# Two output stores cut into transfers of 112, 6, 6 and 4 rows

## The chip, the cores and the metric

The kernel runs on one core of one Trainium2 chip. The metric is the device time of one execution in microseconds. Before the change the median of three runs is 254.41 us (254.31 to 254.42). The profiled execution took 254.46 us; its span on the core, which all times in the trace count from, is 252.7 us, at a mean granted TensorE clock of 0.986 of full speed. Inputs and output lie in the chip's main memory; sixteen DMA engines carry data between it and the core's on-chip memory (128 partitions, one row each).

## The reference

Two stages are fused. The first is attention over channels: for each of four batches, q, k and v are 6400 x 256 in float32, and

```
qn = q / (norm over rows + 1e-6);  kn likewise
s  = kn^T @ qn / tau               # 256 x 256
a  = softmax(s)                    # along the last axis
x  = v @ a                         # 6400 x 256
```

The second is a mixture of eight low-rank adapters on the 25,600 rows of x: `logits = x @ w_gate`, the two largest of eight are chosen for each row and weighted with their softmax, and each chosen adapter e adds `w * ((x @ A[e]) @ B[e])`, of rank 16, to the row. The output is x plus these, 25,600 x 256 in float32, 26.2 MB.

## The kernel before, in words

A batch is called a quarter here. Its 6400 rows are spread over the 128 partitions, 50 consecutive rows to a partition (line 490: `out.rearrange("(b p c) d -> b p c d", b=B, p=P)`). So a column c of 0 to 49 is one chunk of 128 rows, and ten neighbouring columns of one partition are 10,240 consecutive bytes of the output.

**First pass of a quarter.** q and k come in three pieces of 17, 17 and 16 chunks, cast to bfloat16 by the loads themselves (`do_load`, L578, issued from GpSimd). `do_G` (L593, L597, L602) accumulates k^T q and, for part of the chunks, the squared norms in two accumulators on TensorE. For the other chunks ScalarE squares (`do_sq`, L615) and VectorE sums (L621). At the end of a quarter a short serial part makes the softmax: copies of the accumulator (L651), reciprocal root, scaling (L710), exponential on ScalarE (`do_exp`, L715), transposes (`do_aT_ps`, L729), and the products of the attention matrix with the gate and A (L742 to L757).

**Second pass of a quarter.** v comes in five pieces of ten chunks (0 to 4). For a piece, TensorE transposes v (L788), computes the gate and the adapters' first product (L812, or L826 and L879), VectorE makes the top-two weights, the weighted products are transposed (L902), and `do_Y` (L915, L920) accumulates `v @ a` and the adapters' second product for two chunks at a time. `do_Ye` copies each pair into a y tile of 128 x 10 x 256 floats (L769 on ScalarE, L771 on VectorE). There are seven y tiles, used in turn. When a piece is complete, `do_store` (L926) sends its y tile out from SyncE (L928). The last two pieces of the last quarter go in three stores each.

**Order.** A planner (`make_plan`, `Plan.run`) works through all steps with estimated durations and ranks, and writes down an order; the steps are then issued in that order, so each engine carries out its instructions in it and a step that waits holds up what stands behind it. Loads take buffers as they come free. Stores can be held back: `HOLD` (L409) names, for a quarter's piece, a load that must have landed first, and `do_hold` (L645) is a tiny transfer on SyncE that waits for that load. On SyncE the order at the first stores is: piece 2 of quarter 0 (not held), hold on k of quarter 1 piece 2, piece 1, piece 3, hold on k of quarter 3 piece 1, and then the others.

The planner sees a store as one step of fixed cost whatever transfers `do_store` makes of it.

Of the kernel before, what the change touches and what calls it, by code (L numbers as in the profile page):

```python
# [32 lines left out]
class Clock:  # L33


    WINDOW, FIRST, LOW, HIGH = 3.413, 0.31, 0.5, 0.8

# [3 lines left out]
    def at(self, t):  # L41
        w = max(0, int((t - self.FIRST) / self.WINDOW) + 1)
        while len(self.cold) <= w:
            share = self.busy[-1] / self.WINDOW
            self.cold.append(share < (self.HIGH if self.cold[-1] else self.LOW))
            self.busy.append(0.0)
        return w

    def took(self, t, us):

        end, w = t, self.at(t)
        while us > 1e-9:
            pace = 2.0 if self.cold[w] else 1.0
            step = min(us * pace, max(self.FIRST + w * self.WINDOW - end, 1e-6))
            self.busy[w] += step
# [5 lines left out]
    def idle(self, t):  # L61

        w = self.at(t)
        return t - self.FIRST - (w - 1) * self.WINDOW - self.busy[w] > self.SPARE

# [165 lines left out]
def make_plan(B, order, ahead):  # L231
# [150 lines left out]
    for b in range(B):  # L382
        for i in range(NP):
            x = pos["v", b, max(g for g, (i0, _) in enumerate(V) if i0 <= i)]
            parts = UNITS if b == B - 1 and i >= NP - FINE else ((0, PC),)
            for c, n in parts:
# [25 lines left out]

PARTS = {(0, 0): ((0, 2), (2, 15)), (0, 2): ((34, 8), (42, 8)), (3, 2): ((34, 8), (42, 8))}
FINE = 2
FIRST = 4
OFF = {(0, 0, 'k'), (0, 0, 'q'), (0, 1, 'q'), (0, 2, 'k'), (0, 2, 'q'), (0, 4, 'q'), (0, 5, 'q'),
        (0, 6, 'k'), (0, 6, 'q'), (0, 7, 'k'), (0, 8, 'q'), (1, 0, 'k'), (1, 0, 'q'), (1, 1, 'q'),
# [41 lines left out]
def kernel(  # L459
# [11 lines left out]
    nc = tc.nc  # L471

    B, N, C = q.shape
    P = 128
# [15 lines left out]
    out_v = out.rearrange("(b p c) d -> b p c d", b=B, p=P)  # L490
# [44 lines left out]
    held = {}  # L535
# [25 lines left out]
    def do_load(s, what, b, i, c, n):  # L561
        if what == "v":
            t, src, c0 = sb(s, "v", (b, i), [P, PC * max(n for _, n in V), C], BF16), v_v, c
        else:
            t = sb(s, "qk", (what, b, i), [P, max(n for _, n in QK), C], BF16)
            src, c0 = {"q": q_v, "k": k_v}[what], QK[i][0]
            if (b, c) == (0, 0):
                n = FIRST
                if "first" not in W:
# [6 lines left out]
        if (what, b, i) in (("q", 0, 0), ("k", 0, 0)):  # L576
            c, n = FIRST, c + n - FIRST
        nc.gpsimd.dma_start(t[:, c - c0:c - c0 + n, :], src[b, :, c:c + n, :])  # L578
# [346 lines left out]

    def do_store(s, b, i, c, n):  # L926
        lo = i * PC + c
        nc.sync.dma_start(out_v[b, :, lo:lo + n, :], held["y", (b, i), ""][:, c:c + n, :])  # L928


    do = dict(load=do_load, wts=do_wts, sq=do_sq, add=do_add, red=do_red, n2p=do_n2p, hold=do_hold, warm=do_warm, cast=do_cast, G=do_G, accs=do_accs, n2=do_n2, rsqrt=do_rsqrt, rq_ps=do_rq_ps, s=do_s,
              exp=do_exp, recip=do_recip, aT_ps=do_aT_ps, aT=do_aT, waA_ps=do_waA_ps, waA=do_waA,
              a=do_a, ZL=do_ZL, ZLe=do_ZLe, T=do_T, Te=do_Te, log=do_log, loge=do_loge, Z=do_Z, Ze=do_Ze, gzT=do_gzT,
              gzTe=do_gzTe, Y=do_Y, Ye=do_Ye, store=do_store)
    for name in ("m1", "eq1", "lm", "m2", "mask", "msum", "t", "th", "g2"):
        do[name] = gate_step(name)
# [50 lines left out]
```

## Time and profile before

| what | us |
|---|---|
| time, median of three | 254.41 |
| span of the profiled execution | 252.7 |
| TensorE busy | 217.8 (86%) |
| VectorE busy | 192.7 (76%) |
| ScalarE busy | 151.1 (60%) |
| packets of loads, as a share of sixteen DMA engines' span | 74.4% |
| packets of stores and other SyncE transfers, likewise | 26.1% |
| store of a whole piece (1280 KB), median from issue to landing | 16.7 |
| first store of quarter 0 (piece 2), issued | 76.65 |
| then piece 1, and piece 3, issued | 78.40, 89.74 |

How to read it. Busy times are totals over stages with different limits; a share of 86% does not say that the engine bounds every stage. PE is TensorE, DVE is VectorE, ACT is ScalarE, POOL is GpSimd, SP is SyncE. A line such as `ACT ssq L615 <- DMA qk<-in_q_dram: 3.8, 1, 3.8` says that ScalarE stood idle before instructions of line 615 until a DMA landed: 3.8 us in all, once, 3.8 at most. The chain lists start, duration and what ran or was waited for. A line of stretches gives, after the start and end, its length, the busy times of PE, of PE's weight loads, of DVE, ACT and POOL with counts, the granted clock, the mean busy share of the DMA engines and the GB/s they moved. Packets are what a DMA engine handles one after another; a landing is the mark that one DMA engine leaves when its part of a transfer has arrived.

### The profile page before, as it was taken

To read this page: it belongs to the slowest core of one execution; us is meant where nothing else is said; L and a number is where in the kernel's file an instruction comes from. 1 tells how busy PE (TensorE), PEld (TensorE's weight loads), DVE (VectorE), ACT (ScalarE), POOL (GpSimd) and SP (SyncE) were. 2 spreads that over 40 slices of the span, in tenths; PEclk is the share of its full clock that TensorE was granted. 3 is DMA by queue.
4 is the path that set the end of the run, shared out by engine and by line. 5 is a ranking of instruction groups with operands and counts; after the bars stand their busy time and mean duration, and the time that the engine had idled before them with its cause. 6 is when DMAs were issued, how large, how long until landed. Compare 5 with 4: busy or idle time off the path is not lost.

```text
span 252.7 us, 5852 instructions
## 1 busy us (share of the span) xinstructions
PE 217.8 (86%) x2357; PEld 193.0 (76%) x2357; DVE 192.7 (76%) x528; ACT 151.1 (60%) x269; POOL 27.1 (11%) x54
## 2 busy tenths in 40 slices
PE   0274995988999998689999999889999979999990
PEld 0162882876999996579899899779999769999980
DVE  0055589869899987588899899489898898889850
ACT  5454427546786543975667768362674846657671
POOL 7003010040002002000500100500000000000000
PEclk9998899999999999999999999999999999999997
DMA  8999999999999999999999999999999999999996
GB/s 251 217 217 209 211 223 208 217 218 215 215 217 241 303 305 298 224 213 221 210 215 220 215 217 217 211 212 313 317 251 353 322 341 317 337 392 415 404 408 249
DMA packets 11243, 66.70 MB, mean 264 GB/s; under 512 B 1360, under 2 KB 1744, under 8 KB 6608
## 3 DMA queue, kind: packets, MB, share of 16 engines
q0 software_dynamic: 6912, 38.80, 74.4%
q1 hardware_dynamic: 3968, 26.87, 26.1%
q10 hardware_dynamic: 336, 0.66, 0.8%
q8 instruction: 18, 0.29, 0.4%
q14 instruction: 9, 0.07, 0.1%
HBM read 78.91 MB, written 26.21 MB: 416 GB/s over the span
## 4 chain that ended last, share of the span: by engine, by line
PE 53%; DMA 32%; issue 5%; DVE 4%; ACT 2%; POOL 1%; POOLq 0%; DVEq 0%
DMA v<-in_v_dram 18%; PE Y_ps L915 13%; PE acc L593 10%; DMA qk<-in_q_dram 10%; PE Y_ps L920 6%; PE T_ps L788 5%; PE ZL_ps L812 5%; DMA qk<-in_k_dram 5%; PE gzT_ps L902 4%; PE acc L597 3%; PE acc L602 2%; PE Z_ps L879 1%; ACT a_exp L715 1%; DVE a_bf L763 1%; PE log_ps L826 1%
## 5 line engine op out<-in xcount | busy, mean ns | idle before, releaser
L593 PE MATMUL acc<-qk 128*128 128x256 bf16 x400 | 69.6, 282 | 17.0 <-DMA qk<-in_k_dram 9.4
L915 PE MATMUL Y_ps<-a_bf,vT 128*128 128x256 bf16 x400 | 60.0, 273 | 0.2 <-DVE acc_sb L710 0.2
L621 DVE TENSOR_TENSOR ssq<-ssq,sq 128x1280 f32<-128x1280 f32 (+1 forms) x27 | 43.4, 1606 | 19.6 <-ACT sq L615 19.6
L769 ACT COPY y<-Y_ps 128x512 f32<-128x512 f32 x79 | 46.2, 586 | 16.6 <-PE Y_ps L920 13.5
L593 PEld LDWEIGHTS <-qk 128*128 128x128 bf16 x400 | 34.2, 101 | 20.7 <-DMA qk<-in_k_dram 11.5
L615 ACT ACTIVATE sq<-qk 128x1280 f32<-128x1280 bf16 (+1 forms) x27 | 36.9, 1368 | 17.7 <-DVE ssq L621 16.6
L915 PEld LDWEIGHTS <-vT 128*128 128x128 bf16 x400 | 38.9, 98 | 4.7 <-issue 0.3
L920 PE MATMUL Y_ps<-ball,gzT 128*128 128x256 bf16 x200 | 38.2, 273 | 0.0
L597 PE MATMUL acc<-qk 128*128 128x128 bf16 x242 | 34.5, 224 | 0.0
L788 PE MATMUL T_ps<-ident,v 128*128 128x128 f32 x200 | 27.6, 274 | 0.6 <-DVE waA_sb L757 0.4
L769 ACT COPY vT<-T_ps 128x512 f32<-128x512 f32 (+1 forms) x44 | 21.2, 510 | 10.9 <-PE T_ps L788 10.5
L597 PEld LDWEIGHTS <-qk 128*128 128x128 bf16 x242 | 24.4, 101 | 3.5
L890 DVE TENSOR_TENSOR gz<-zl,gateg 128x256 bf16<-128x256 f32 x70 | 26.3, 445 | 0.3
L578 POOL DMA_DIRECT2D v<-in_v_dram x20 | 11.5, 576 | 133.7 <-PE T_ps L788 92.8
L788 PEld LDWEIGHTS T_ps<-ident,v 128*128 128x128 f32 x200 | 22.3, 141 | 1.6 <-DVE waA_sb L757 0.6
L602 PE MATMUL acc<-qk 128*128 128x128 bf16 x168 | 23.4, 222 | 0.0
L902 PE MATMUL gzT_ps<-ident,gz 128*128 128x128 f32 x100 | 20.9, 281 | 2.6 <-DVE gateg L868 1.4
L920 PEld LDWEIGHTS <-gzT 128*128 128x128 bf16 x200 | 19.6, 98 | 2.3
L812 PE MATMUL ZL_ps<-waA_sb,vT 128*128 128x136 bf16 x280 | 19.5, 223 | 1.7 <-DVE waA_sb L757 1.5
L771 DVE COPY gzT<-gzT_ps 128x256 f32<-128x256 f32 (+1 forms) x40 | 15.0, 380 | 7.1 <-PE gzT_ps L902 5.6
L812 PEld LDWEIGHTS <-vT 128*128 128x128 bf16 x280 | 17.7, 98 | 2.4 <-issue 2.1
L615 ACT ACTIVATE ssq<-qk 128x1536 f32<-128x1536 bf16 x8 | 11.9, 1489 | 11.4 <-DMA qk<-in_q_dram 7.4
(80 smaller groups left out, 271.3 us busy)
## 6 DMA issues: line engine op xcount, KB each, us to landing
out_dram<-y SPq DMA_DIRECT2D x18, 1280.0 KB, 16.7
v<-in_v_dram POOLq DMA_DIRECT2D x20, 640.0 KB, 20.5
qk<-in_q_dram POOLq DMA_DIRECT2D x7, 1088.0 KB, 23.7
qk<-in_k_dram POOLq DMA_DIRECT2D x7, 1088.0 KB, 28.4
qk<-in_q_dram POOLq DMA_DIRECT2D x4, 512.0 KB, 19.2
qk<-in_k_dram POOLq DMA_DIRECT2D x4, 512.0 KB, 22.5
qk<-in_q_dram POOLq DMA_DIRECT2D x2, 1024.0 KB, 19.4
qk<-in_k_dram POOLq DMA_DIRECT2D x2, 1024.0 KB, 23.8
```

The source lines that it names most:

```text
L593: nc.tensor.matmul(acc[ic][:, 0:256], kt[:, j, ic::CC], qt[:, j, :], start=c == 0, stop=False, skip_group_check=True)
L597: nc.tensor.matmul(acc[ic][:, 256:384], kt[:, j, ic::CC], kt[:, j, ic::CC], start=False, stop=False, skip_group_check=True)
L602: nc.tensor.matmul(acc[ic][:, 384:512], qt[:, j, ic * P:(ic + 1) * P], qt[:, j, ic * P:(ic + 1) * P], start=False, stop=c == NC - 1, skip_ ...
L615: nc.scalar.activation(out[:, 0:n, :], t[:, j:j + n, :], ACT.Square)
L621: nc.vector.tensor_tensor(out=t, in0=t, in1=held["sq", (w, b, g), ""][:, 0:n, :], op=OP.add)
L769: nc.scalar.copy(out, in_)
L788: nc.tensor.matmul(ps[:, j, :], vt[:, c + j, :].bitcast(FP32), W["ident32"], is_transpose=True, start=(j == 0), stop=(j == n - 1))
L812: nc.tensor.matmul(ps[:, j, :], vT_of(b, i, c + j)[:, :, ic], st[b]["waA"][:, ic, :], start=(j == 0 and ic == 0), stop=(j == n - 1 and ic ...
L890: nc.vector.tensor_tensor(out=pairs[:, h].rearrange("p c (e r) -> p c e r", e=E), in0=z[:, 2 * h:2 * h + 2, :].rearrange("p c (e r) -> p c ...
L902: nc.tensor.matmul(ps[:, j, :], pairs[:, j * P:(j + 1) * P], W["ident32"], is_transpose=True, start=(j == 0), stop=(j == n // 2 - 1))
L915: nc.tensor.matmul(ps[:, j, :], vT_of(b, i, c + j)[:, :, ic], st[b]["a"][:, ic, :], start=(j == 0 and ic == 0), stop=False, skip_group_che ...
L920: nc.tensor.matmul(ps[:, j, :], pair[:, :, j], W["B"], start=False, stop=(j == 1), skip_group_check=True)
```

## The change

Two stores of quarter 0, those of pieces 2 and 3, are each issued as four transfers: partitions 0 to 111, 112 to 117, 118 to 123 and 124 to 127. All other stores stay one transfer of 128 partitions. The same bytes go to the same places. The purpose is to alter how the rows of these two stores are shared out among the sixteen DMA engines.

```diff
 FINE = 2
+SPLIT, SHARES = {(0, 2), (0, 3)}, (112, 6, 6, 4)
 FIRST = 4
...
     def do_store(s, b, i, c, n):
         lo = i * PC + c
-        nc.sync.dma_start(out_v[b, :, lo:lo + n, :], held["y", (b, i), ""][:, c:c + n, :])
+        p = 0
+        for rows in SHARES if (b, i) in SPLIT else (P,):
+            nc.sync.dma_start(out_v[b, p:p + rows, lo:lo + n, :], held["y", (b, i), ""][p:p + rows, c:c + n, :])
+            p += rows
```

## The prediction

> **What bounds the kernel now.** First the page: the busy shares, the slices and the queues.
>
> ```profile
> PE 217.8 (86%) x2357; PEld 193.0 (76%) x2357; DVE 192.7 (76%) x528; ACT 151.1 (60%) x269; POOL 27.1 (11%) x54
> ...
> DMA  8999999999999999999999999999999999999996
> GB/s 251 217 217 209 211 223 208 217 218 215 215 217 241 303 305 298 224 213 221 210 215 220 215 217 217 211 212 313 317 251 353 322 341 317 337 392 415 404 408 249
> ...
> q0 software_dynamic: 6912, 38.80, 74.4%
> q1 hardware_dynamic: 3968, 26.87, 26.1%
> q8 instruction: 18, 0.29, 0.4%
> ```
>
> The DMA engines are busy in every slice from start to end; loads (q0) and stores (q1) add up to 100% of sixteen engines. TensorE follows at 86%. Slices 13 to 16 (76 to 101 us) stand out before 170 us with up to 305 GB/s: there the first three output pieces leave between loads. Second, the waits between 60 and 150 us, and the chain there:
>
> ```profile
> ACT ssq L615 <- DMA qk<-in_q_dram: 3.8, 1, 3.8
> ...
> PE aT_ps L729 <- ACT a_exp L715: 2.2, 1, 2.2
> ```
>
> ```profile
> 77.04 24.46 DMA qk<-in_q_dram
> 101.49 0.02 issue
> 101.52 1.48 ACT ssq L615
> 103.00 0.83 ACT a_exp L715 x2
> 103.83 0.05 issue
> 103.88 0.28 PE aT_ps L729 x2
> ```
>
> One load, q of quarter 2 piece 0, is issued at 77.04 and lands at 101.49. A squaring of ScalarE waits for it; the exponential of quarter 1 stands behind that squaring in the queue, and TensorE behind the exponential. It is the only DMA wait of over 0.7 us on a computing engine after 60 us. Third, the stretches at the end and the last pieces of the chain:
>
> ```profile
> 205.00:239.00 34.00, 32.55 (x396) 30.17 (x394) 29.77 (x99) 21.63 (x49) 1.03 (x2) 1.00 1.01 367
> 239.00:247.00 8.00, 7.77 (x71) 6.64 (x68) 4.20 (x13) 5.64 (x11) 0.00 (x0) 1.00 0.98 401
> ```
>
> ```profile
> 246.55 0.23 PE Y_ps L920 x2
> 246.78 0.02 issue
> 246.81 0.59 ACT y L769
> ```
>
> TensorE works to 246.78 and the DMA engines stay full (1.01, then 0.98): two limits run side by side. Which ends last is in the landing records: each transfer leaves sixteen, one for each DMA engine, without its number. The last store, issued at 247.42, lands first at 249.95 and last at 251.95. The first engines had nothing queued (2.53 us from issue); the latest had 2.00 us of older work before it. So **the end hangs on the latest DMA engine**, and TensorE has 2 us of room against it.
>
> Read through the run, these spreads show a steady skew. The v load issued at 53.27 lands over 79.13 to 81.20: twelve engines within 0.86 us, then 1.20, 1.26, 1.90 and 2.07. For q of quarter 2 the latest are 2.41, 3.10 and 3.28 after the first (98.22). For the large store issued at 233.23 the delays are 0, 0.26, 0.36, 0.45, 0.80, 1.10, then eight from 1.87 to 3.09, then 3.81 and 3.95. Six engines are early, two late. Lateness comes in jumps: the q8 packet at 30.37 (0.97 us) is followed by one engine of sixteen going from within 0.65 to 1.57.
>
> **What the skill says.** (1) "DMA: Bandwidth & Descriptors", "Why a DMA increments its semaphore by 16 and not by 1": a transfer uses k engines, the largest k up to 16 that divides its slowest dimension, on the SyncE path the lowest-numbered k. So 112 rows use all sixteen, seven rows each; 6 rows the engines 0 to 5; 4 rows 0 to 3. Every transfer before has sixteen landings; none shows a smaller k. (2) Same page, "Queues, rings and completion order": an engine alternates between the queues that hold work, packet by packet. The trace agrees: near 82 us packets of 5,120 bytes (v) and 10,240 bytes (store) take turns, 0.773 us a pair. (3) "Runtime: NRT & Kernel Launch", "Instruction fetch mechanics": instructions come by DMA in 16 KiB blocks; the trace has 18 packets of 16,384 bytes, 0.89 to 0.99 us each, the source of the jumps. (4) First page, "Latency and other measured facts": engines 7 and 15 are usually the slower ones. The trace has two latest engines, with no numbers to them.
>
> **The change part by part.** *Bytes:* none added. One row is one packet of 10,240 bytes; eight take 3.06 us (first landings at 232.63 and 235.69 of two stores), so 0.382 us each. Per split store, engines 0 to 3 get 7+1+1+1 = 10 rows instead of 8, engines 4 and 5 get 9, engines 6 to 15 get 7. For two stores: engines 0 to 3 **+4 rows, +1.53 us**; 4 and 5 +0.76; 6 to 15 **-2 rows, -0.76 us**.
>
> *Issues:* six more on SyncE at 0.33 to 0.58 us (the duration range of its store issues), about 2.2 us. Three delay the hold at 77.75 and the store at 78.40 by some 1.1 us; q1 still holds piece 2 until the landings at 86 to 88 us, so its rings stay fed. Three follow the store at 89.74; after them stands only the next hold, whose load lands at 166.87. Hidden both times. The new waits for a reused semaphore, by the order of instructions, are on transfers landed long before, or for the last small ones on piece 2 (87.7, wanted after 90). The compute copies that reuse a y buffer get four waits for one, on stores landed by about 106; those buffers are filled again only with later quarter 1 pieces. Zero. Six more completion writes of 0.02 us or less each: zero. The other engines keep their instruction order.
>
> *The load at 101.49:* stringing packets into sixteen rows (each starts where one ended), the two latest engines finish this load at 101.14 and 100.97, and at those same instants their last packet of quarter 0's stores. All 24 store packets lay ahead of it. With 22, the load ends 0.76 earlier there. The next engine lands at 100.63, store packets still waiting: alternation goes on, so rows more or fewer behind it do not move it. Landing 101.49 - 0.76 = 100.73, still later than 100.63. The squaring, exponential and TensorE move by the same 0.76: the 2.2 us wait shrinks. If the latest two are among engines 0 to 5, the load stays at 101.49, no worse.
>
> *Later loads:* k of quarter 2 piece 0 lands at 106.96 and is used by TensorE at 109.75; the v load landing at 110.0 is used at 113.06. On a loaded engine they come up to 1.53 later, inside 2.8 and 3.1 us. Beyond 110 us no computing engine waits over 0.7 us for a load.
>
> *The end:* between the last two large stores the latest landings lie 3.04 us apart (242.68, 245.72), the price of eight rows: no pause on the latest engine, where the first ones lie 4.63 apart. So its end moves by what its work moves. If the two latest (3.95, 3.81) are in 6 to 15: 251.95 - 0.76 = 251.19. Engines 0 to 3, if they are the early ones (up to 0.45), rise to 1.98; 4 and 5 (1.10) to 1.86; the middle falls to 2.33; the latest is 3.19 and still sets the end. Both limits move by 0.76, and TensorE had 2 us of room anyway.
>
> The unknown price is which engines are late. Its bounds: all late ones relieved, -0.76; the latest loaded, +1.53. I take -0.76: the skill puts the slow engines at 7 and 15, both relieved; the same handful stays early from 125 us on (four or five within 0.47), so lateness is not passed round evenly.
>
> **Rivals.** *A middle engine takes over:* one of engines 0 to 3 is from the group at 2.26 to 2.6. It rises to 3.8 to 4.1 against the old 3.95: -0.15 to +0.2, time 254.3 to 254.6, no change. For it: eight of sixteen are in the middle. Against: lowest-numbered engines would have to be spread over the groups. *A late engine is loaded (slower):* middle at 3.09 gives 4.62, +0.67, 255.1; the latest at 3.95 gives 5.48, +1.53, 255.9. For it: no record names an engine; if lateness were strewn at random, four loaded engines would seldom all miss the late ten. Against: the early group persists. *Hidden anyway:* TensorE's chain gains nothing and its tail sets the end: 254.4. Against it: the 2.00 us of queue on the latest engine at the last store.
>
> **How the numbers follow.** Forecast, late engines relieved: 254.41 - 0.76 = 253.65, say 253.7, chance 0.58. No change (middle engine or hidden) 0.20, at 254.3 to 254.6. Slower 0.22, of which 0.13 near 255.1 and 0.09 near 255.9. Range: a little under the full gain, 253.4, for packets that run otherwise in small transfers, up to 255.1, which leaves out the worst. Faster by over 0.2% (0.51 us) is below 253.90: the forecast, 0.58; slower is above 254.92: 0.22.
>
> **What would show it.** Right: q of quarter 2 lands near 100.7, the ScalarE wait shrinks from 3.8 to about 3.0, the large store near 233 us has its latest landing some 3.2 us after the old first one, and the last store's spread is below 2.0. Wrong: that spread grows with a single group of four late engines; or the load stays at 101.5; or the 112-row transfer's packets take longer than 0.40 us; or the 6-row transfers land on sixteen engines.

## The result, and the profile after

After the change the kernel takes 255.49 us (median of four runs, 255.41 to 255.56) against 254.41 before (four runs, 254.31 to 254.47). The ratio is 1.0043, with a 95% interval of 1.0025 to 1.006: slower by about 1.1 us. The forecast was 253.7, and the range ended at 255.1.

First the page of the kernel after the change: busy shares, slices, queues.

```profile
PE 217.7 (86%) x2357; PEld 192.7 (76%) x2357; DVE 192.8 (76%) x528; ACT 151.3 (60%) x269; POOL 27.0 (11%) x54
...
DMA  8999999999999999999999999999999999999994
GB/s 253 212 217 211 214 222 210 215 218 213 217 215 255 300 299 284 234 219 217 210 215 221 216 214 218 211 212 317 313 260 356 342 324 319 335 403 425 399 408 173
...
q1 hardware_dynamic: 4000, 26.87, 26.0%
q8 instruction: 18, 0.29, 0.4%
q14 instruction: 9, 0.07, 0.1%
```

The engines' work and the stores' bytes are as before; q1 has 32 packets more, which carry no data to speak of. What differs stands in the last slice: a DMA share of 4 tenths and 173 GB/s, where it was 6 tenths and 249. The kernel ends with most DMA engines idle. The stretches after the last matmul show how many are left at work. Before the change (the columns are those of the earlier table of stretches; the last two are the DMA share and GB/s):

```profile
247.00:250.00 3.00, 0.00 (x0) 0.00 (x0) 0.00 (x0) 0.39 (x1) 0.00 (x0) 0.86 0.96 383
250.00:251.50 1.50, 0.00 (x0) 0.00 (x0) 0.00 (x0) 0.00 (x0) 0.00 (x0) 0.50 0.27 104
251.50:254.00 2.50, 0.00 (x0) 0.00 (x0) 0.00 (x0) 0.00 (x0) 0.00 (x0) 0.50 0.00 1
```

And after it, with the two stretches that were shown of before at the head:

```profile
205.00:239.00 34.00, 32.55 (x395) 30.16 (x393) 29.77 (x100) 21.52 (x48) 0.91 (x2) 1.00 1.01 366
239.00:247.00 8.00, 7.65 (x69) 6.54 (x66) 4.08 (x13) 5.75 (x11) 0.00 (x0) 1.00 0.98 405
...
247.00:250.00 3.00, 0.00 (x0) 0.00 (x0) 0.00 (x0) 0.27 (x1) 0.00 (x0) 1.00 0.94 374
250.00:251.50 1.50, 0.00 (x0) 0.00 (x0) 0.00 (x0) 0.00 (x0) 0.00 (x0) 0.98 0.21 83
251.50:254.00 2.50, 0.00 (x0) 0.00 (x0) 0.00 (x0) 0.00 (x0) 0.00 (x0) 0.50 0.03 10
```

Until 247 us next to nothing has changed in these sums. After 251.5 a share of 0.03 of sixteen engines over 2.5 us is 1.2 us of work: one engine, busy alone to the end. The sixteen landings of the last store (issued at 247.42 before, 247.29 after) say the same:

```
before: 249.95 249.96 249.96 249.97 249.97 250.10 250.32 250.40 250.67 250.74 251.02 251.02 251.10 251.15 251.75 251.95
after:  249.83 249.84 249.87 249.91 249.94 249.96 249.99 250.07 250.20 250.36 250.76 250.93 251.06 251.16 251.35 252.91
```

Fifteen engines are done by 251.35, which is 0.60 before the old end. One comes at 252.91, 0.96 after it. TensorE had nothing to do with it; its last matmuls end at 246.66, where they ended at 246.78:

```profile
246.43 0.23 PE Y_ps L921 x2
246.66 0.02 issue
246.68 0.59 ACT y L770
```

The other part of the forecast, the load of q of quarter 2, can be read in the waits of 60 to 150 us and the chain there:

```profile
ACT ssq L616 <- DMA qk<-in_q_dram: 2.9, 1, 2.9
PE aT_ps L730 <- ACT a_exp L716: 1.4, 1, 1.4
```

```profile
77.01 23.63 DMA qk<-in_q_dram
100.64 0.02 issue
100.67 1.48 ACT ssq L616
102.15 0.83 ACT a_exp L716 x2
102.98 0.05 issue
103.03 0.28 PE aT_ps L730 x2
```

It lands at 100.64 instead of 101.49, and TensorE goes on at 103.03 instead of 103.88, as forecast. But the 0.85 us does not last. Between 160 and 175 us ScalarE now waits 2.4 us for a later load of q (0.7 before), and the chain of 155 to 200 us hangs on a load of k, which lands at 183.80 (182.94 before):

```profile
ACT sq L616 <- DMA qk<-in_q_dram: 2.4, 1, 2.4
```

```profile
159.91 1.55 POOL qk L579 x3
161.46 22.34 DMA qk<-in_k_dram
183.85 0.39 PE acc L594 x2
```

So both gains that were forecast were there: the two latest engines became earlier, and the first load landed earlier. A third thing outweighed them: one engine that was not the latest became so, by a wide margin.

### The profile page after: what moved, and what is told of

It reads as the page before. It is cut to its first block, busy times and chain, and to the rows that moved or that the text cites. A ratio compares the mean times of both kernels' runs of the same rounds, so it can differ in the third digit from the quotient of the medians.

```text
span 253.7 us, 5862 instructions
## 1 busy us (share of the span) xinstructions
PE 217.7 (86%) x2357; PEld 192.7 (76%) x2357; DVE 192.8 (76%) x528; ACT 151.3 (60%) x269; POOL 27.0 (11%) x54
## 4 chain that ended last, share of the span: by engine, by line
PE 45%; DMA 40%; issue 6%; DVE 3%; ACT 2%; POOL 1%; POOLq 0%; DVEq 0%
DMA v<-in_v_dram 17%; DMA qk<-in_k_dram 14%; PE Y_ps L916 12%; DMA qk<-in_q_dram 9%; PE acc L594 7%; PE Y_ps L921 6%; PE T_ps L789 5%; PE ZL_ps L813 4%; PE gzT_ps L903 4%; PE acc L598 2%; PE acc L603 1%; PE Z_ps L880 1%; POOL qk L579 1%; ACT a_exp L716 1%; PE log_ps L827 1%
```

## The experiments

The ratios below are to runs of the kernel before that were taken beside each kernel (medians 254.34 to 254.40 us); landings are those of one profiled execution each.

The theory after the result: one of the engines 0 to 3, which carry four rows more, was already nearly the latest. Rivals: the three more transfers of each split store (issues, completion writes) cost time by themselves; or the load on any low-numbered engine costs it.

**Splitting without shifting, and even sharing.** Two kernels split the same stores so that each engine gets the eight rows per store that it had before.

```diff
-SPLIT, SHARES = {(0, 2), (0, 3)}, (112, 6, 6, 4)
+SPLIT, SHARES = {(0, 2), (0, 3)}, (112, 16)            # first kernel
+SPLIT, SHARES = {(0, 2), (0, 3)}, (32, 32, 32, 32)     # second kernel
```

> Both stores go as 112 + 16 rows: two transfers each on all sixteen DMA engines, 7 + 1 rows to an engine, so every engine carries what it carried before the change. Theory (the end is set by the work of the latest DMA engine; with the change that is one of the loaded engines 0 to 3): no change from before, 254.3 to 254.6, load of q of quarter 2 at 101.5, last landing at 252.0. Rival, more transfers and issues cost: a third of the six extra ones, +0.36, 254.8. Rival, rows of a 112-row transfer run slower than those of a 128-row one: the whole +1.08, 255.5.

> Both stores go as four transfers of 32 rows, each on all sixteen engines: as many issues and completions as the change or more, but 8 rows to every engine as before. Theory: no change from before, 254.3 to 254.6. Rival, issues and completions cost: +1.08, 255.5. Rival, 112-row transfers are slow: 254.4.

Measured: 254.74 us for 112 and 16 rows (ratio 1.0015, 1.0008 to 1.0021) and 254.46 us for four times 32 (1.0004, 0.9996 to 1.0012). Four transfers of equal shares cost nothing that can be measured, so it is not the number of transfers. The 0.3 us of 112 and 16 is above the theory's range and nearer to the rival's 254.8, while its last landing (251.82) is not later than before (251.95). That rest comes after the last landing; the ledger below finds it there. In the waits of the kernel with four times 32:

```profile
ACT ssq L616 <- DMA qk<-in_q_dram: 2.4, 1, 2.4
...
PE aT_ps L730 <- ACT a_exp L716: 0.9, 1, 0.9
```

Here the load of q of quarter 2 lands at 100.02, earlier still than after the change, and TensorE's last matmul ends at 245.86, 0.9 us before that of the kernel before. The time stays the same. TensorE's chain does not set the end, then; and the early landing of that load does not need the two missing rows, since no engine has fewer rows here.

**More or fewer rows on the low engines.**

```diff
-SPLIT, SHARES = {(0, 2), (0, 3)}, (112, 6, 6, 4)
+SPLIT, SHARES = {(0, 2), (0, 3)}, (112, 8, 8)          # engines 0 to 7: +2 rows in all
+SPLIT, SHARES = {(0, 2), (0, 3)}, (112, 4, 4, 4, 4)    # engines 0 to 3: +6 rows in all
```

> Both stores as 112 + 8 + 8 rows: engines 0 to 7 get 9 rows a store (+0.76 us over two), engines 8 to 15 get 7 (-0.76). Theory: the loaded engine that set the end with +1.53 (last landing 252.9) now carries 0.76 less, so its last landing is 252.1 and the time 254.5 to 254.7, if none of the late engines is number 6 or 7; if one is, its 251.95 becomes 252.7 and the time 255.2, and the load of q of quarter 2 may stay at 101.5. Rival, issues cost: four of six extra, 255.1. Rival, slow 112-row transfers: 255.5.

> Both stores as 112 + 4 + 4 + 4 + 4 rows: engines 0 to 3 get 11 rows a store (+2.29 us over two), engines 4 to 15 get 7 (-0.76). Theory: the engine that sets the end with the change gets 0.76 more, last landing 253.7, time 256.2 to 256.4; the load of q of quarter 2 lands at 100.6 as with the change, so TensorE's part at 104 us is early although the end is later. Rival, issues cost: eight extra against six, 255.8. Rival, the end follows the computing chain: no later than with the change.

Measured: 254.62 us (1.0012, 1.0004 to 1.002) and 256.21 us (1.0076, 1.0062 to 1.0089). The end of the second, in its stretches:

```profile
250.00:251.50 1.50, 0.00 (x0) 0.00 (x0) 0.00 (x0) 0.00 (x0) 0.00 (x0) 0.79 0.26 102
251.50:254.00 2.50, 0.00 (x0) 0.00 (x0) 0.00 (x0) 0.00 (x0) 0.00 (x0) 0.50 0.05 20
```

0.05 of sixteen engines over 2.5 us is 2.0 us, again about one engine alone; the last two landings are 252.23 and 253.52, and the other fourteen are in by 251.15. From four rows more on engine 3 (the change, 252.91) to six (253.52) the last landing moves by 0.61 us, 0.3 us a row where a packet's price is 0.382.

**Each store alone.**

```diff
-SPLIT, SHARES = {(0, 2), (0, 3)}, (112, 6, 6, 4)
+SPLIT, SHARES = {(0, 2)}, (112, 6, 6, 4)    # first kernel
+SPLIT, SHARES = {(0, 3)}, (112, 6, 6, 4)    # second kernel
```

> Only piece 2 of quarter 0 goes as 112 + 6 + 6 + 4 rows. Theory (work of the latest engine): the engine that sets the end with the change carries +0.76 instead of +1.53, last landing 252.0 to 252.2, time 254.5 to 254.7: most of the loss is gone, not half of it, since the unloaded late engines end at 251.6 to 252.0 anyway. Rival (each split store costs by itself): half of the loss, 254.95.

> Only piece 3 of quarter 0 goes as 112 + 6 + 6 + 4 rows. Theory: as with piece 2 alone, 254.5 to 254.7. Rival (each split store costs by itself, and the one that runs beside more loads costs more): about 254.95, and different from piece 2 alone.

Measured: 254.81 us (1.0019, 1.0012 to 1.0026) and 254.76 us (1.0016, 1.001 to 1.0023). Both lie just above the theory's range and below the rival's 254.95. The two differ by less than their intervals, so which store is split does not matter. Their loss of 0.35 to 0.40 us is mostly not that of the rows: 112 and 16, which moves no row, loses 0.33 as well, and all three lose 0.31 to 0.37 us after the last landing (the ledger below). So two rows more cost little (last landings 252.22 and 251.70, against 251.95) and four rows 0.96 us: the loaded engine had some room. An estimate of it from the landings is 1.53 - 0.96 = 0.57 us for four rows, and 2.29 - 1.57 = 0.72 us for six.

**Which engine is which.** A kernel gives nearly every engine another number of rows. Each packet of an engine starts where its last one ended, so the packets of the trace can be strung into sixteen rows, and the counts of output packets then give each string its engine. The numbers rest on the rule that the prediction takes from the Trainium skill in its first point, that a transfer of fewer engines takes the lowest-numbered ones; were it another order, the names would change and not the argument.

```diff
-SPLIT, SHARES = {(0, 2), (0, 3)}, (112, 6, 6, 4)
+SPLIT = {(0, 2): (96, 11, 6, 5, 4, 3, 2, 1), (0, 1): (64, 15, 14, 13, 12, 10), (0, 3): (96, 9, 8, 8, 7)}
...
-        for rows in SHARES if (b, i) in SPLIT else (P,):
+        for rows in SPLIT.get((b, i), (P,)):
```

> Three stores of quarter 0 (pieces 2, 1 and 3) are cut so that no two DMA engines get the same rows: 96+11+6+5+4+3+2+1, 64+15+14+13+12+10 and 96+9+8+8+7. A transfer of k rows below 16 uses engines 0 to k-1, so the rows that an engine carries tell its number in the trace. Not meant to be fast: engine 0 gets 8 rows more than before (+3.06 us), engine 15 eight fewer. Theory: the 8,192-byte instruction packets go to engines among 0 to 3 and the 16,384-byte ones to eight engines of which at most one is among 0 to 5; time 255.5 to 257. Rival (lateness is passed round all engines): instruction packets on every engine.

Measured: 256.12 us in one run. The instruction packets, strung up to 165 us, lie so:

```
16,384 bytes (q8): 30.1 engine 13, 48.7 engine 14, 61.4 engine 5, 76.1 engine 6, 85.4 engine 9, 96.3 engine 10,
                   111.5 engine 11, 121.4 engine 12, 136.8 engine 13, 147.3 engine 14, 158.0 engine 5
8,192 bytes (q14): 50.9, 106.1, 158.4 engine 3; 72.9, 157.0 engine 1; 145.9 engine 2
none:              engines 0, 4, 7, 8, 15
```

(Strung on to 173 us, the row counts leave only engine 9 for the packet at 85.4, and the next large one, at 171.3, is on engine 6.) The large ones go round eight engines, 5, 6 and 9 to 14, beginning at 13. If the order holds to the end, eighteen packets over eight engines make three for engines 13 and 14 and two for the other six. Each takes 0.89 to 0.97 us here, and up to 1.25 in the other kernels. The small ones take 0.31 to 0.43 us and come back to engine 3. Of the engines 0 to 3 it has the most of them. Strung up in the same way, the change shows engine 3 at 158 us 4.33 us behind the earliest engine, and engines 0, 1 and 2 only 2.63 to 3.11; in the kernel with four times 4 rows engine 3 is at 4.91 and the other three at 3.14 to 4.27, the last of them engine 1 just after a small packet. The ten engines 6 to 15, which carry equal rows in the change, show what a large packet does: three that had none are 0.00, 0.19 and 0.34 us behind at 158 us, five that had one 1.30 to 1.89, two that had two 2.37 and 2.59. From 149 to 157 us an engine that has no instruction packet keeps its lag to 0.01 us. Engine 5, with two large packets and two rows more, is at 4.02, next to engine 3.

**Engine 3 against its neighbours.** If engine 3 alone is the trouble, engines 0 to 2 can take four rows more without loss, and moving a single row per store from engine 3 to engine 0 must give most of the loss back.

```diff
-SPLIT, SHARES = {(0, 2), (0, 3)}, (112, 6, 6, 4)
+SPLIT, SHARES = {(0, 3)}, (112, 3, 3, 3, 3, 3, 1)         # first kernel
+SPLIT, SHARES = {(0, 2), (0, 3)}, (112, 6, 6, 3, 1)       # second kernel
```

> Only piece 3 is split, into transfers of 112, 3, 3, 3, 3, 3 and 1 rows. Engine 0 gets 5 rows more than in the kernel before (+1.91 us at 0.382 us a row), engines 1 and 2 get 4 more (+1.53 us, as engine 3 does in the change), engines 3 to 15 get one row less (-0.38 us). Theory, that engine 3 alone is late among the low ones because instruction packets run on it: engine 3 is relieved, engines 0 to 2 have the room, the last landing stays at or before 251.95 and the time is 254.0 to 254.6. Rival, that four more rows on any of the low-numbered engines are what costs: the last landing is about 252.9 and the time 255.3 to 255.8.

> The change with one row of each store moved: 112, 6, 6, 3 and 1 rows. The fourth row of engine 3 goes to engine 0; all other engines carry what they carry in the change. Over both stores, against the kernel before: engine 0 +6 rows (+2.29 us), 1 and 2 +4 (+1.53), 3 to 5 +2 (+0.76), 6 to 15 -2 (-0.76). Theory, that engine 3 sets the end after the change: two rows less on it and the end is 0.76 us earlier, unless engine 0 comes in its place with 2.29 us: 254.6 to 254.9. Rival, that it's the load on the low-numbered engines as a group, or the splitting itself: 255.4 to 255.9.

Measured: 254.21 us (0.9995, 0.9987 to 1.0003), last landing 251.56; and 254.60 us (1.0007, 0.9999 to 1.0016), last landing 251.78. Both fall where the theory put them (the second at its lower edge) and 0.8 us or more from the rivals. The second kernel differs from the change in two rows, one of each split store, and is 0.89 us faster; 0.11 us of that comes after the last landing (the ledger). Its end, in the stretches:

```profile
250.00:251.50 1.50, 0.00 (x0) 0.00 (x0) 0.00 (x0) 0.00 (x0) 0.00 (x0) 1.00 0.28 111
251.50:254.00 2.50, 0.00 (x0) 0.00 (x0) 0.00 (x0) 0.00 (x0) 0.00 (x0) 0.53 0.00 0
```

The lone engine after 251.5 us is gone.

**Relieving the engines that are late.** With the map, shares can be chosen that take rows from engines 13 to 15 and give them to 0 to 2, and leave engine 3 as it is.

```diff
-SPLIT, SHARES = {(0, 2), (0, 3)}, (112, 6, 6, 4)
+SPLIT, SHARES = {(0, 2), (0, 3)}, (112, 13, 3)            # first kernel
+SPLIT, SHARES = {(0, 1), (0, 2), (0, 3)}, (112, 13, 3)    # second kernel
```

> Both pieces go as 112, 13 and 3 rows. Engines 0 to 2 get two rows more over both stores (+0.76 us), engines 3 to 12 the same as in the kernel before, engines 13 to 15 two rows less (-0.76 us). Theory, that engines 13 and 14 land last before the change and engine 3 is the one that the change made late: the last landing falls to 251.2 to 251.5 and the time to 253.7 to 254.1, below both kernels. Rival, that the end is not set by the landing of engines 13 and 14: 254.4 to 254.8, as with 112 and 16 rows.

> 112, 13 and 3 rows on pieces 1, 2 and 3. Against the kernel before, engines 0 to 2 get three rows more (+1.15 us), 3 to 12 the same, 13 to 15 three less (-1.15 us). Theory: with two pieces so split the last landings are already those of the middle group (251.02, 251.04 and 251.09), which this does not relieve, so no further gain: 253.8 to 254.2. Rival, that engines 13 and 14 still set the end: 0.38 us less, 253.5 to 253.8.

Measured: 254.02 us (0.9988, 0.9982 to 0.9995) and 253.92 us (0.9983, 0.9977 to 0.999). Both are faster than either kernel, by 0.4 us against the one before and 1.5 us against the change. The stretches of the first:

```profile
247.00:250.00 3.00, 0.00 (x0) 0.00 (x0) 0.00 (x0) 0.00 (x0) 0.00 (x0) 1.00 0.91 365
250.00:251.50 1.50, 0.00 (x0) 0.00 (x0) 0.00 (x0) 0.00 (x0) 0.00 (x0) 0.54 0.16 61
251.50:254.00 2.50, 0.00 (x0) 0.00 (x0) 0.00 (x0) 0.00 (x0) 0.00 (x0) 0.50 0.00 0
```

Its last store lands last at 251.09 and has nine landings from 250.49 to 251.09: a group, no longer two stragglers. That landing is a little earlier than the 251.2 that the theory gave at the least. A third piece brings no more than 0.1 us, within the intervals. A third kernel went too far:

```diff
-SPLIT, SHARES = {(0, 2), (0, 3)}, (112, 6, 6, 4)
+SPLIT = {(0, 2): (112, 13, 3), (0, 1): (112, 3, 3, 3, 3, 3, 1), (0, 3): (112, 13, 3)}
...
-        for rows in SHARES if (b, i) in SPLIT else (P,):
+        for rows in SPLIT.get((b, i), (P,)):
```

> Pieces 2 and 3 go as 112, 13 and 3 rows and piece 1 as 112, 3, 3, 3, 3, 3 and 1. Against the kernel before, engine 0 gets 7 rows more (+2.67 us), engines 1 and 2 six more (+2.29 us), engines 3 to 12 one less (-0.38 us), engines 13 to 15 three less (-1.15 us). Theory: as long as engines 0 to 2 have that much room, the end falls by a further 0.2 to 0.4 us against 112, 13 and 3 alone, to 253.4 to 253.9. If engine 1 or 2, which carry a few instruction packets, has less room than 2.3 us, the time goes up to 254.5 to 255.5.

Measured: 255.47 us (1.0045, 1.0032 to 1.0059), the case of too little room. One engine again lands alone, at 252.34, with the other fifteen in by 251.08; at 158 us the latest of all is engine 1 or 2 (the two carry alike), 4.34 us behind.

**A ledger.** Most of the landings can be worked out afterwards from two terms. Take for each engine its instruction packets (0.95 us a large one, 0.32 a small one) and its rows against the kernel before (0.382 us each). Packets later than the strung-up part are assumed: the large ones go on in their order (three on 13 and 14, two on the other six), and the last three small ones are put on engine 3 (six on it, two on 1, one on 2). So the sums are an estimate, 2.85 us for engines 13 and 14 before, 1.92 for engine 3. Much hangs on those last three: with the three small packets that were mapped engine 3 would have 2.49 us in the change, below 2.85. The landings speak for them: at 158 us of the change engine 3 is only 0.31 us behind engine 5, which gets no further large packet in this order, and the last landing comes 1.56 us behind all others. So the last engine took on at least 1.25 us after 158 us, about three small packets. The largest sum in each kernel, against the old 2.85:

| kernel | engine with the largest sum | sum | less 2.85 | last landing, against 251.95 | from it to the end of the span | time |
|---|---|---|---|---|---|---|
| before | 13, 14 | 2.85 | 0 | 251.95 | 0.72 | 254.41 |
| four times 32 | 13, 14 | 2.85 | 0 | 251.73, -0.22 | 0.85 | 254.46 |
| 112, 16 | 13, 14 | 2.85 | 0 | 251.82, -0.13 | 1.09 | 254.74 |
| 112, 8, 8 | 3: 1.92 + 0.76 | 2.68 | -0.17 | 251.78, -0.17 | 0.97 | 254.62 |
| 112, 6, 6, 3, 1 | 3: 1.92 + 0.76 | 2.68 | -0.17 | 251.78, -0.17 | 0.74 | 254.60 |
| 112, 6, 6, 4 on piece 2 alone | 3: 1.92 + 0.76 | 2.68 | -0.17 | 252.22, +0.27 | 1.04 | 254.81 |
| 112, 6, 6, 4 on piece 3 alone | 3: 1.92 + 0.76 | 2.68 | -0.17 | 251.70, -0.25 | 1.03 | 254.76 |
| the change | 3: 1.92 + 1.53 | 3.45 | +0.60 | 252.91, +0.96 | 0.84 | 255.49 |
| 112, four times 4 | 3: 1.92 + 2.29 | 4.21 | +1.36 | 253.52, +1.57 | 0.74 | 256.21 |
| the map | 3: 1.92 + 1.91 | 3.83 | +0.98 | 253.55, +1.60 | 0.74 | 256.12 |
| engines 0 to 2 loaded | 13, 14: 2.85 - 0.38 | 2.47 | -0.38 | 251.56, -0.39 | 0.84 | 254.21 |
| 112, 13, 3 twice | 13, 14: 2.85 - 0.76 | 2.09 | -0.76 | 251.09, -0.86 | 0.97 | 254.02 |
| 112, 13, 3 on three pieces | 3: 1.92 (13, 14: 1.70) | 1.92 | -0.93 | 251.04, -0.91 | 0.84 | 253.92 |
| too far | 1: 0.64 + 2.29 | 2.93 | +0.08 | 252.34, +0.39 | 1.10 | 255.47 |

It gives the sign of every step larger than 0.3 us, and the size to within 0.45 us, but for the map with 0.6. Where a loaded low engine clearly sets the end it comes out 0.2 to 0.6 too small; what adds that is open.

The column before the time shows why kernels that land 0.1 to 0.25 us earlier than before can still be slower. At the end SyncE asks for the semaphores of the transfers, one after another in a fixed order, and its transfers take these semaphores in turn. So the number of transfers decides where in that order the last store stands. SyncE's last checks, with the number of the semaphore behind each start:

```
before (last store 118, landed 251.95):  ... 250.09 (116) 251.32 (117) 251.97 (118)
112, 16 (last store 108, landed 251.82): ... 251.21 (107) 251.84 (108) 251.90 (109) 251.97 (110)
                                             252.02 (111) 252.09 (116) 252.15 (117) 252.21 (118)
```

Each check behind the last store's takes 0.06 us. There are none in the kernel before, two in the change, and six with 112 and 16. Landing and checks together give the profiled executions: -0.13 + 0.37 = +0.24 for 112 and 16 (254.72 against 254.46 us), +0.96 + 0.12 = +1.08 for the change (255.56). The others come out within 0.05 us, but for "too far", which takes 0.24 us more.

## Why the prediction was wrong

*What bounds the kernel:* right. The end hangs on the latest DMA engine and TensorE has room: two kernels whose TensorE is done 0.9 and 1.0 us earlier than before (four times 32, and 112 and 16: 245.86 and 245.74) are not faster, and the lone engine is seen in the stretches of the slow ones.

*Bytes and rows:* right. The small transfers leave six, six and four landings, besides a mark some 0.5 us after their issue (for the first store six at 86.60 to 87.25, six at 87.59 to 88.41, four at 88.90 to 89.57), which agrees with the Trainium skill, "DMA: Bandwidth & Descriptors", "Why a DMA increments its semaphore by 16 and not by 1"; and the packets of the map can be strung up on that rule. Nearly all packets of 10,240 bytes take 0.385 to 0.398 us in the shared stretch of 78 to 88 us, in both kernels.

*Issues and completions at zero:* held for the stores themselves; four times 32 rows, with the same number of transfers, is no slower. Left out was that the added transfers move the last store's place among SyncE's final checks, 0.12 us here.

*The load at 101.49:* forecast 100.73, measured 100.64. The size was right by luck. With 32 rows four times no engine lost a row, and the load came at 100.02. And of the two engines that finished this load last before the change, the later one is the engine of the large packet at 59.0 us, which is engine 5 on the map: the change gave it two rows more. By the prediction's own working ("If the latest two are among engines 0 to 5, the load stays at 101.49") nothing should have been gained. Strung up, that engine finished the load at 101.14 with all 24 of its store packets ahead of it before the change, and at 100.15 with 22 ahead and four behind it after. So the store packets came later in relation to the load. Why is open: a completion packet of each added transfer may take a store's turn in the alternation with the load, which is argued and was not separated. The gain was given back at 160 to 184 us, where no engine had waited over 0.7 us for a load before, and would not have moved the end anyway.

*The end:* here the step failed that put the late engines: "I take -0.76: the skill puts the slow engines at 7 and 15, both relieved". Half of it came true. The two latest engines were among 6 to 15 and were relieved: without the lone straggler the end is 251.35, where 251.19 was forecast. But they are most likely 13 and 14, with two large instruction packets each by 158 us and a third if the order holds; engines 7 and 15, which the page calls usually slower ("Latency and other measured facts"), carried no instruction packet in the map, and no run showed them late. (With 13 to 15 alike in rows, in the kernel that went too far, two of the three carry the large packets and the third is the earliest of all at 158 us.) The measurement decides. And to relieve the latest was only half of the question. The other half, whether one of the four engines that got 1.53 us was late as well, was answered with the early group: "Engines 0 to 3, if they are the early ones (up to 0.45), rise to 1.98". Engines 0 to 2 fit that loosely, engine 3 not at all. Its last landing was some 251.38 before, an estimate (252.91 less 1.53): only 0.57 us ahead of the latest, where it got 1.53.

*The rivals:* what came is "A late engine is loaded": a middle engine at 3.09 of the large store's spread, forecast at +0.67 and 255.1, measured at +0.96 in the landing and +1.08 in time. The neighbouring rival, "A middle engine takes over", took a middle engine at 2.26 to 2.6 and so found no change. What it named as speaking against it ("lowest-numbered engines would have to be spread over the groups") is what happened: the small instruction packets spread them. The trace of before held the sign of it, nine q14 packets of 8,192 bytes at 50 to 246 us, and the prediction counted only the eighteen of q8.

*What would show it:* the sign named for wrong was a group of four late engines. It was one, since three of the four had room.

## What to carry to other kernels

Here all DMA engines were full almost to the end, the kernel ended with its latest engine, and the mean share hid it. In such a case read the landings of the last store, and the DMA share of the stretch after the last matmul, as a count of engines still at work. Before rows are moved between engines, make a ledger for each engine that receives some, instruction packets of every queue included; the room of the fullest receiver, not that of the group, set how much could be moved. When transfers are added, look also at what stands between the last landing and the end. A kernel whose shares differ for each engine tells which engine is which in a single run. It showed here that 13 and 3 rows after 112 take 0.4 us off, where 6, 6 and 4 add 1.1.

## What the runs showed of the hardware

- Instruction packets make DMA engines late: in the change, engines of equal rows are 0 to 0.34, 1.30 to 1.89 and 2.37 to 2.59 us behind at 158 us after none, one and two large ones. The large ones (16,384 bytes, 0.89 to 1.25 us) went to engines 13, 14, 5, 6, 9, 10, 11, 12 in turn, the small ones (8,192 bytes, 0.31 to 0.43 us) to 3, 1 and 2, most often 3. The Trainium skill, "Runtime: NRT & Kernel Launch", "Instruction fetch mechanics", tells of blocks of 16 KiB; those of q8 agree, those of q14 are half as large.
- A lag between DMA engines that are never idle is kept, to 0.01 us from 149 to 157 us. What the stores issued at 77 to 91 us laid on engine 3 (1.53 us) was still there at the end: its last landing came 0.96 us after the old one.
- More transfers for the same bytes did not slow the stores: three more for each of two stores, 254.46 against 254.41 us. But they move the last store's place in SyncE's final checks of semaphores, at 0.06 us a check: 0.72 to 1.10 us from the last landing to the end of the span.
